# A small routed group gathered into 64 columns, ahead of a dynamic loop over (chunk, expert) pairs

## The chip, the cores and the metric

One Trainium2 chip, and of it one core. The metric is the device time of one execution in microseconds (us). The kernel before was timed in three runs, 638.36, 639.25 and 640.91 us; their median is 639.25 us.

The core has engines that run beside each other, each with its own instruction stream in fixed order: TensorE (PE, with its weight loads as PEld), VectorE (DVE), ScalarE (ACT), GpSimd (POOL) and SyncE (SP), which issues nearly all DMAs. They wait for each other through semaphores.

## The reference

Three stages in a row, all in fp32, with N = 1152 rows (2 batches of 576) of 512 values:

- *Attention with random features.* For each of 2 x 8 heads, q and k (576 x 64) go through `exp(x @ omega.T - |x|^2/2 - max)`, then `num = q_p @ (k_p.T @ v)`, `den = q_p @ sum(k_p) + 1e-6`, and the output is `num / den`. The heads side by side give a matrix x of 1152 x 512.
- *Routed experts, 8 of them.* Each row takes the one expert with the largest logit: `e = argmax(x @ w_gate)`. Its output is `gate * sigmoid(x @ w_output_gate)[e] * (relu(x @ w1[e]) @ w2[e])`, with `gate` the softmax value of e, w1 512 x 1024 and w2 1024 x 512.
- *Dense experts, 4 of them.* All rows go through all four, and the four outputs are added with weights `p = domain_probs / sum`.

Which expert a row takes is known only when the logits are there, so this is decided on the chip.

## The kernel before, in words

Values are split into a rounded part and the rest, both in the type fp32r ("rounded fp32", one pass on TensorE), and a product is made of three matmuls: high x high, high x low, low x high (`mm3`, L558). Matmuls on plain fp32 tiles (the transposes, the attention products, the gate row in `gate_row`) take two passes each in the records.

*Attention* (to about 117 us) runs by hand-written software stages over (batch, half of the heads). `stage_d` (L336) makes one normalised tile `xn` of up to 128 rows x 256 values on VectorE (L351), transposes it on TensorE (L354) and puts it, split, into `xh` and `xl`, where the 1152 rows lie as columns. There are 20 such calls. The tiles hold every fourth row of a batch, put in the order `SLOT_J`; the last 64 rows of a batch are a "rest" tile.

*Routed experts.* The 1152 columns are four chunks of 288, two for each batch: 256 from two tiles and 32 from the rest tile. For each batch the expert that most rows take is its main expert, and each chunk goes through the main expert of its batch whole, columns of other rows being multiplied with zero by the gate row. One chunk through the first layer is `unit1` (8 x 4 x 3 = 96 matmuls of 288 columns), through the second `unit2` (4 x 8 x 3 = 96 matmuls); results go to `x2T`, 512 x 1152. `extras` (L649) makes, on VectorE, the list of all other (chunk, expert) pairs that have at least one row, with their number `nx`, the experts `le` and chunks `lc`, and for each a mask in `mt`. A dynamic loop (L701 to L721) then makes one trip for each pair: the whole chunk of 288 columns through the pair's expert, with a gate row that is zero for all other rows, added to `x2T`. The order is: unit1 and unit2 of chunk 0, unit1 of chunk 1, unit2 of chunk 1, the loop, then chunks 2 and 3.

*Weights.* An expert's layer is loaded by two DMAs of 1 MB each on SP into staging tiles `st`, of which there are two in all, and split into 8 pairs of tiles (`whi` by ScalarE at L90, `wlo` by VectorE or GpSimd at L91). There are 8 tile pairs for the first layer and 8 for the second, so a tile of the next expert is split when the last matmul of the former expert has read it. The first-layer weights for the loop's first trip are asked for ahead of unit2 of chunk 1 (L694 to L696); a trip loads its own second layer and the first layer of the next trip, and the last trip loads that of batch 1's main expert. Where there is no pair, the index at L694 is that of batch 1's main expert.

*Dense experts* (from about 252 us) follow with products of 320 and 256 columns and of 512 columns, and run to the end.

*What sets the order.* The instructions are written in the order of the code, but a scheduler fixes each engine's stream before the run: at a modelled time it issues to each engine the first instruction in code order that is ready, as far as tiles of a pool are free. So instructions of later code fill modelled gaps. Nothing is moved across the bounds of the dynamic loop.

Of the kernel before, what the change touches and what calls it, by code (L numbers as in the profile page):

```python
# [9 lines left out]
F32 = mybir.dt.float32  # L10
# [12 lines left out]
DM = 512  # L23
# [6 lines left out]
HBUFS = 4  # L30
GROUPS = ((0, 320), (640, 256))
LAG, LAGD = 3, 5
EB, FLIP = 6, 1
MXS = 8
SCALE = 1.0 / (D ** 0.25)
# [4 lines left out]
def moe_stack(ctx, tc, q, k, v, omega, w_gate, w_ogate, mw1, mw2, dprobs, dw1, dw2, out):  # L40
# [3 lines left out]
    def f32(ap):  # L44
        return ap.bitcast(F32)
# [110 lines left out]
    def load_group(b, hh, cut=1):  # L156
# [7 lines left out]
        if (b, hh) == (0, 0):  # L164
            raw["q", 2] = load_rest(q, "qr")

    om2 = cp.tile([128, 2, D], F32, name="om2")
    for r in range(2):
        nc.scalar.dma_start(om2[:, r, :], omega)
# [21 lines left out]
    wgh = cp.tile([128, KB, 16], F32R, name="wgh")  # L191
    wgl = cp.tile([128, KB, 16], F32R, name="wgl")

    def prep_late():
        TT(fold, ident[:, 0:32], ident[:, 32:64], op=ALU.add)
        TT(fold, fold, ident[:, 64:96], op=ALU.add)
        TT(fold, fold, ident[:, 96:128], op=ALU.add)
        nc.vector.tensor_reduce(cmask, ident.rearrange("p (c r) -> p c r", r=32), axis=AX.X, op=ALU.add)
        nc.gpsimd.iota(i32, pattern=[[1, 32]], base=0, channel_multiplier=0)
        nc.vector.tensor_copy(iota, i32)  # L200
        TS(iota1, iota, 1.0, None, op0=ALU.add)
        TS(rev, iota[:, 0:NE], -1.0, float(NE), op0=ALU.mult, op1=ALU.add)
        nc.vector.tensor_copy(ue, iota[:, 0:NE].unsqueeze(1).to_broadcast([128, 4, NE]))
        nc.vector.tensor_copy(uc, iota[:, 0:4].unsqueeze(2).to_broadcast([128, 4, NE]))
        nc.vector.memset(lgr, 0.0)
        split(wgh, wgl, wg)
        ds_ = cp.tile([128, 9], F32, name="ds_")
        nc.vector.tensor_reduce(ds_, dpr, axis=AX.X, op=ALU.add)
        TS(ds_, ds_, 1e-9, None, op0=ALU.add)
        nc.vector.reciprocal(ds_, ds_)  # L210
        TT(pb, dpr, ds_.unsqueeze(2).to_broadcast([128, 9, NE2]), op=ALU.mult)
# [124 lines left out]
    def stage_d(b, hh, u):  # L336
# [10 lines left out]
        rd = ap.tile([128, G], F32, tag="rd", name="rd", bufs=4)  # L347
        TS(rd[:m], ps[:m, :, D], M * 1e-6, None, op0=ALU.add)
        nc.vector.reciprocal(rd[:m], rd[:m])
        xn = ap.tile([128, G, D], F32, tag="xn", name="xn")  # L350
        TT(xn[:m], ps[:m, :, 0:D], rd[:m].unsqueeze(2).to_broadcast([m, G, D]), op=ALU.mult)  # L351
        px = bank[:, 0:256].rearrange("p (g n) -> p g n", g=2)
        for g in range(2):
            nc.tensor.transpose(px[:, g, :m], xn[:m, 2 * g:2 * g + 2, :].rearrange("p a d -> p (a d)"), ident[:m, :m])  # L354
# [270 lines left out]
    def dyn(w, e):  # L625
        return w[bass.ds(e, 1)].rearrange("o a b -> (o a) b")
# [22 lines left out]
    def extras():  # L649
# [10 lines left out]
        for i, sft in enumerate((1, 2, 4, 8, 16)):  # L660
            dst = (pa, pb_)[i % 2]
            nc.vector.tensor_copy(dst[:, 0:sft], src[:, 0:sft])
            TT(dst[:, sft:32], src[:, sft:32], src[:, 0:32 - sft], op=ALU.add)
            src = dst
        nx = cp.tile([128, 1], I32, name="nx")
        nc.vector.tensor_copy(nx, src[:, 31:32])
        mine = cp.tile([128, 32], F32, name="mine")
# [4 lines left out]
        TT(mv, src.unsqueeze(1).to_broadcast([128, 32, 32]), iota1.unsqueeze(2).to_broadcast([128, 32, 32]),  # L672
           op=ALU.is_equal)
        lists = []
        for nm, tab in (("le", ue), ("lc", uc)):
            t = lp.tile([128, 32, 32], F32, tag="lt", name="lt", bufs=1)
            TT(t, mv, tab.rearrange("p c e -> p (c e)").unsqueeze(1).to_broadcast([128, 32, 32]), op=ALU.mult)
            s = cp.tile([128, 32], F32, name=nm + "f")
            nc.vector.tensor_reduce(s, t, axis=AX.X, op=ALU.add)
# [2 lines left out]
            si = cp.tile([128, 32], I32, name=nm)  # L682
            nc.vector.tensor_copy(si, s)
            lists.append(si)
        return nx, mt, lists[0], lists[1]

    E0.load2((nc.vector, nc.gpsimd))
    unit2(0, E0.w2, hs)
    nx_t, mt, le_t, lc_t = extras()
    hs = unit1(1, E0.w1)  # L690
    for c in (2, 3):
        for cols in x2cols(c):
            nc.gpsimd.memset(x2T[:, :, cols], 0.0)
    e = nc.values_load(le_t[0:1, 0:1], engines=[SP], min_val=0, max_val=NE - 1)  # L694
    E1 = Expert(dyn(mw1, e), None, nc.vector)
    E1.load1()  # L696
    unit2(1, E0.w2, hs)


    nx = nc.values_load(nx_t[0:1, 0:1], min_val=0, max_val=28)  # L700
# [238 lines left out]
```

## Time and profile before

| | us |
|---|---|
| median of the three timed runs | 639.25 |
| the profiled execution, its own time | 637.48 |
| its span in the trace | 635.7 |
| VectorE busy | 422.4 |
| ScalarE busy | 263.2 |
| GpSimd busy | 259.9 |
| mean granted TensorE clock (share of full) | 0.995 |

The span is that of one profiled execution, and lies 1.78 us under that execution's time. Busy shares are means over stages with different limits, so they say little of one stage. TensorE's matmuls overlap in the records (a record of 0.29 us may be followed by the next after 0.13 us), so the step from one start to the next is what a matmul costs, not its duration. A timeline row gives the start, the time, the engine, the line, what is written and read, the number of merged instructions, and in brackets how long the engine had been idle and what ended that.

### The profile page before, as it was taken

Reading aid. Unit: us, or ns where it says so; the run is one execution under the profiler, and the core shown is the slowest. Engines: PE = TensorE matmul, PEld = TensorE weight load, DVE = VectorE, ACT = ScalarE, POOL = GpSimd, SP = SyncE. Lnnn points to the kernel's source line nnn. Section 1 sums busy time; section 2 is a strip of 40 time slices with the busy share of each in tenths; the row PEclk is TensorE's granted clock in tenths of the full one; section 3 lists DMA queues with packets and bytes.
Section 4 is the critical chain, followed back from the end, with each engine's and each line's share of the span. In section 5 each row is a group of like instructions: output and inputs, shape, how many; then the busy total and the mean of one; then the engine's idle time right before and its main releaser. Section 6 shows DMA issues by size and latency. Waiting matters only on the chain.

```text
span 635.7 us, 10767 instructions
## 1 busy us (share of the span) xinstructions
PE 615.7 (97%) x3985; PEld 565.4 (89%) x3986; DVE 422.4 (66%) x953; ACT 263.2 (41%) x632; POOL 259.9 (41%) x297
## 2 busy tenths in 40 slices
PE   7989989899999999899999999999999999999997
PEld 6879889799998999789899899899899898898995
DVE  7677576885284478976756656666667666666564
ACT  5567474414062244544433433433343343442230
POOL 4994032500000001367636646646645745744220
PEclk9999998999999999999999999999999999999999
DMA  8711033005243302201202202102201102200004
GB/s 200 188 35 34 2 139 128 2 6 194 68 132 132 135 1 66 67 2 51 83 1 67 67 0 68 68 1 66 68 2 66 67 1 68 67 1 1 2 0 148
DMA packets 38180, 39.60 MB, mean 62 GB/s; under 512 B 14448, under 2 KB 26736, under 8 KB 38128
## 3 DMA queue, kind: packets, MB, share of 16 engines
q1 hardware_dynamic: 37840, 38.85, 19.6%
q8 instruction: 31, 0.51, 0.3%
q14 instruction: 21, 0.17, 0.1%
q10 hardware_dynamic: 288, 0.07, 0.0%
HBM read 36.55 MB, written 2.36 MB: 61 GB/s over the span
## 4 chain that ended last, share of the span: by engine, by line
PE 87%; DVE 5%; DMA 3%; ACT 2%; issue 1%; SPq 1%; POOL 0%; DVEq 0%; ACTq 0%
PE po L561 10%; PE po L560 10%; PE po L562 10%; PE pp L560 9%; PE pp L561 9%; PE pp L562 9%; PE py L560 3%; PE py L562 3%; PE py L561 3%; PE kv L297 3%; PE ph L562 3%; PE ph L560 3%; PE ph L561 3%; PE pnd L345 2%; DMA st<-in_moe_w_dram 1%
## 5 line engine op out<-in xcount | busy, mean ns | idle before, releaser
L91 POOL TENSOR_TENSOR wlo<-st,whi 128x512 fp32r<-128x512 f32 x100 | 121.5, 1236 | 243.2 <-ACT whi L90 238.9
L884 DVE SCALAR_TENSOR_TENSOR oacc<-po,pb,oacc 128x512 f32<-128x512 f32 x135 | 100.1, 748 | 56.5 <-PE po L562 56.4
L90 ACT CAST whi<-st 128x512 fp32r<-128x512 f32 x144 | 82.0, 598 | 134.2 <-PE po L562 49.3
L560 PE MATMUL po<-whi,hh 128*128 128x512 f32 x288 | 112.5, 391 | 0.0
L561 PE MATMUL po<-wlo,hh 128*128 128x512 f32 x288 | 112.4, 390 | 0.0
L562 PE MATMUL po<-whi,hl 128*128 128x512 f32 x288 | 111.9, 389 | 0.0
L556 POOL TENSOR_TENSOR hl<-c,hh 128x320 fp32r<-128x320 f32 (+1 forms) x64 | 52.5, 820 | 87.7 <-ACT hh L555 75.0
L560 PE MATMUL pp<-xh,whi 128*128 128x320 f32 (+1 forms) x256 | 75.7, 296 | 0.2 <-DVE u L843 0.2
L562 PE MATMUL pp<-xh,wlo 128*128 128x320 f32 (+1 forms) x256 | 75.8, 296 | 0.0
L561 PE MATMUL pp<-xl,whi 128*128 128x320 f32 (+1 forms) x256 | 75.7, 296 | 0.0
L562 PEld LDWEIGHTS po<-whi,hl 128*128 128x128 f32 x288 | 54.1, 188 | 11.4
L560 PEld LDWEIGHTS po<-whi,hh 128*128 128x128 f32 x288 | 54.1, 188 | 10.5
L561 PEld LDWEIGHTS po<-wlo,hh 128*128 128x128 f32 x288 | 54.1, 188 | 10.0
L831 DVE TENSOR_TENSOR c<-u,pp 128x320 f32<-128x320 f32 (+1 forms) x96 | 43.3, 453 | 22.2 <-PE pp L562 21.8
L560 PEld LDWEIGHTS pp<-xh,whi 128*128 128x128 f32 x256 | 48.5, 190 | 1.7 <-DVE u L843 0.5
L554 ACT ACTIVATE c<-c 128x320 f32<-128x320 f32 (+1 forms) x64 | 28.5, 445 | 51.3 <-DVE c L831 50.5
L561 PEld LDWEIGHTS pp<-xl,whi 128*128 128x128 f32 x256 | 48.5, 190 | 1.2
L560 PE MATMUL ph<-xh,whi 128*128 128x288 f32 (+1 forms) x160 | 47.8, 299 | 1.5 <-issue 1.5
L562 PEld LDWEIGHTS pp<-xh,wlo 128*128 128x128 f32 x256 | 48.5, 190 | 0.0
L560 PE MATMUL py<-hh,whi 128*128 128x288 f32 x160 | 48.5, 303 | 0.0
L562 PE MATMUL ph<-xh,wlo 128*128 128x288 f32 (+1 forms) x160 | 48.1, 301 | 0.0
L561 PE MATMUL ph<-xl,whi 128*128 128x288 f32 (+1 forms) x160 | 47.5, 297 | 0.0
(217 smaller groups left out, 1406.1 us busy)
## 6 DMA issues: line engine op xcount, KB each, us to landing
st<-in_moe_w_dram SPq DMA_DIRECT2D x32, 512.0 KB, 4.4
st<-in_moe_w_dram SPq DMA_DIRECT2D x12, 1024.0 KB, 5.3
v<-in_v_dram SPq DMA_DIRECT2D x16, 128.0 KB, 3.4
q<-in_q_dram SPq DMA_DIRECT2D x4, 512.0 KB, 4.7
out_dram<-oacc SPq DMA_DIRECT2D x8, 256.0 KB, 2.1
k<-in_k_dram SPq DMA_DIRECT2D x3, 512.0 KB, 5.2
k<-in_k_dram SPq DMA_DIRECT2D x4, 128.0 KB, 2.4
kr<-in_k_dram SPq DMA_DIRECT2D x2, 128.0 KB, 3.4
```

Of the source, the lines that this page charges most:

```text
L90: nc.scalar.copy(hi, src)
L91: eng.tensor_tensor(lo, src, f32(hi), op=ALU.subtract)
L297: nc.tensor.matmul(kvps[key][:, i, :], e[i][r0:r1], v65[i], start=first and i == 0, stop=last and i == G - 1)
L345: nc.tensor.matmul(ps[:m, i, :], t[:, i, c0:c0 + m], kvs[b, hh][:, i, :], start=True, stop=True)
L554: nc.scalar.activation(c, c, AF.Relu)
L556: nc.gpsimd.tensor_tensor(hl, c, f32(hh), op=ALU.subtract)
L560: nc.tensor.matmul(ps, sh_, mh, start=start, stop=False)
L561: nc.tensor.matmul(ps, sh_, ml, start=False, stop=False)
L562: nc.tensor.matmul(ps, sl_, mh, start=False, stop=stop)
L831: TT(c, u, p, op=op)
L884: STT(oacc[:, T], po, pc, oacc[:, T], op0=ALU.mult, op1=ALU.add)
```

## The change

The 20 tiles `xn` are written to a DRAM buffer `xs` too, by DMAs on SP, and `xn` has four buffers in place of two. `extras` takes the first pair out of the list where it has at most 64 rows: the list and `nx` are then shorter by one, and a mask `sel1` and the indices of its expert and chunk come back. For this pair the kernel asks for the expert's weights, reads the chunk's three stored tiles back (rows on partitions), gives every row of the pair a slot number from a running count (a matmul with an upper triangle), and gathers the rows into 64 columns by matmuls with one-hot matrices. The first layer runs with 128 moving columns, 64 high and 64 low parts side by side, so that two matmuls in place of three give a product; the second layer has these 128 columns as stationary side. The 64 results are put back to their columns, with the gate factors, by matmuls with the transposed one-hot matrices, and added to `x2T`. This stands in the code after unit1 of chunk 1 and ahead of its unit2 up to the first layer, and after it from the second layer on. The request for the first layer of the next expert (`E1.load1`) moves behind all of this. The loop itself is as it was.

```diff
+SLOTS = 64
+    xs = ctx.enter_context(tc.tile_pool(name="dp", bufs=1, space=bass.MemoryType.DRAM)).tile([9, 128, DM], F32, name="xs")
...
+    slot = cp.tile([128, SLOTS], F32, name="slot")
+    upper = cp.tile([128, 128], F32, name="upper")
+
+    def prep_slots():
+        si = cp.tile([128, 128], I32, name="si")
+        nc.gpsimd.iota(si, pattern=[[1, 128]], base=0, channel_multiplier=0)
+        nc.gpsimd.tensor_copy(slot, si[:, 0:SLOTS])
+        ui = cp.tile([128, 128], I32, name="ui")
+        nc.gpsimd.iota(ui, pattern=[[1, 128]], base=0, channel_multiplier=-1)
+        nc.gpsimd.tensor_copy(upper, ui)
+        nc.gpsimd.tensor_scalar(upper, upper, 0.0, None, op0=ALU.is_gt)
+
     def prep_late():
+        prep_slots()
...
-        xn = ap.tile([128, G, D], F32, tag="xn", name="xn")
+        xn = ap.tile([128, G, D], F32, tag="xn", name="xn", bufs=4)
         TT(xn[:m], ps[:m, :, 0:D], rd[:m].unsqueeze(2).to_broadcast([m, G, D]), op=ALU.mult)
+        dst = xs[8, 64 * b:64 * b + 64] if rest else xs[4 * b + SLOT_J[u[3]]]
+        nc.sync.dma_start(dst[:, 256 * hh:256 * hh + 256], xn[:m].rearrange("p g d -> p (g d)"))
...
+        sel = cp.tile([128, 32], F32, name="sel1")
+        STT(sel, src, 1.0, flat, op0=ALU.is_equal, op1=ALU.mult)
+        sc = cp.tile([128, 32], F32, name="sc")
+        TT(sc, sel, cnt.rearrange("p c e -> p (c e)"), op=ALU.mult)
+        few = cp.tile([128, 2], F32, name="few")
+        nc.vector.tensor_reduce(few[:, 0:1], sc, axis=AX.X, op=ALU.add)
+        TS(few[:, 0:1], few[:, 0:1], SLOTS + 0.5, None, op0=ALU.is_lt)
+        TS(few[:, 1:2], src[:, 31:32], 0.5, None, op0=ALU.is_gt)
+        TT(few[:, 0:1], few[:, 0:1], few[:, 1:2], op=ALU.mult)
+        TS(sel, sel, few[:, 0:1], None, op0=ALU.mult)
+        TT(flat, flat, sel, op=ALU.subtract)
+        TS(src, src, few[:, 0:1], None, op0=ALU.subtract)
+        where = cp.tile([128, 2], F32, name="where")
+        for i, tab in enumerate((ue, uc)):
+            TT(sc, sel, tab.rearrange("p c e -> p (c e)"), op=ALU.mult)
+            nc.vector.tensor_reduce(where[:, i:i + 1], sc, axis=AX.X, op=ALU.add)
+        wi = cp.tile([128, 2], I32, name="wi")
+        nc.vector.tensor_copy(wi, where)
...
+        pool_t = ExitStack()
+        ltp = pool_t.enter_context(tc.tile_pool(name="ltp", bufs=1))
         for nm, tab in (("le", ue), ("lc", uc)):
-            t = lp.tile([128, 32, 32], F32, tag="lt", name="lt", bufs=1)
+            t = ltp.tile([128, 32, 32], F32, tag="lt", name="lt")
...
-        return nx, mt, lists[0], lists[1]
+        pool_t.close()
+        return nx, mt, lists[0], lists[1], sel.rearrange("p (c e) -> p c e", c=4), wi
...
-    nx_t, mt, le_t, lc_t = extras()
+    nx_t, mt, le_t, lc_t, sel1, wi_t = extras()
     hs = unit1(1, E0.w1)
...
+    pool_x = ExitStack()
+    xg_ = pool_x.enter_context(tc.tile_pool(name="xg", bufs=1))
+    ex = nc.values_load(wi_t[0:1, 0:1], engines=[SP], min_val=0, max_val=NE - 1)
+    cx = nc.values_load(wi_t[0:1, 1:2], engines=[SP, DVE], min_val=0, max_val=3)
+    X = Expert(dyn(mw1, ex), dyn(mw2, ex), nc.vector)
+    X.load1()
+    xt = [xg_.tile([128, DM], F32, tag="xt", name="xt", bufs=3) for _ in range(3)]
+    for t in range(2):
+        nc.sync.dma_start(xt[t], xs[bass.ds(cx * 2 + t, 1)].rearrange("o p d -> (o p) d"))
+    nc.sync.dma_start(xt[2], xs[8])
+
+    def picked(nm, main, rest):
+
+        v = xg_.tile([128, 3], F32, name=nm)
+        t = xg_.tile([128, 4, 2, NE], F32, tag="pk", name="pk")
+        TT(t, main[:, 0:8].rearrange("p (c t) e -> p c t e", t=2),
+           sel1.unsqueeze(2).to_broadcast([128, 4, 2, NE]), op=ALU.mult)
+        nc.vector.tensor_reduce(v[:, 0:2], t.rearrange("p c t e -> p t c e"), axis=AX.XY, op=ALU.add)
+        t2 = xg_.tile([128, 4, NE], F32, tag="pk2", name="pk2")
+        TT(t2, rest, sel1, op=ALU.mult)
+        nc.vector.tensor_reduce(v[:, 2:3], t2, axis=AX.XY, op=ALU.add)
+        return v
+
+    mask, fac = picked("mask", oh_all, ohr), picked("fac", g_all, grm)
+    pr = ps_n.tile([128, 2, 3], F32, tag="nd", name="pr")
+    nc.tensor.matmul(pr[:, 0], upper, mask, start=True, stop=True)
+    nc.tensor.matmul(pr[:, 1], ones, mask, start=True, stop=True)
+    rank = xg_.tile([128, 2, 3], F32, name="rank")
+    nc.vector.tensor_copy(rank, pr)
+    for t in (1, 2):
+        for i in range(t):
+            TT(rank[:, 0, t:t + 1], rank[:, 0, t:t + 1], rank[:, 1, i:i + 1], op=ALU.add)
+    og = xg_.tile([128, 3, SLOTS], F32, name="og")
+    ogf = xg_.tile([128, 3, 2, SLOTS], F32, name="ogf")
+    for t in range(3):
+        TS(og[:, t], slot, rank[:, 0, t:t + 1], mask[:, t:t + 1], op0=ALU.is_equal, op1=ALU.mult)
+        for i in range(2):
+            TS(ogf[:, t, i], og[:, t], fac[:, t:t + 1], None, op0=ALU.mult)
+    px = ps_n.tile([128, KB, SLOTS], F32, tag="nd", name="px")
+    for kb in range(KB):
+        for t in range(3):
+            nc.tensor.matmul(px[:, kb], xt[t][:, 128 * kb:128 * kb + 128], og[:, t], start=t == 0, stop=t == 2)
+    xg = xg_.tile([128, KB, 2, SLOTS], F32R, name="xg")
+    nc.scalar.copy(xg[:, :, 0], px)
+    TT(xg[:, :, 1], px, f32(xg[:, :, 0]), op=ALU.subtract)
+    psx = ps_t.tile([128, 3, 128], F32, tag="pt", name="psx")
+    for t in range(3):
+        nc.tensor.transpose(psx[:, t], ogf[:, t].rearrange("p a s -> p (a s)"), ident)
+    back = xg_.tile([128, 3, 128], F32, name="back")
+    nc.scalar.copy(back, psx)
+
+    hx = xg_.tile([128, FB, 2, SLOTS], F32R, name="hx")
+    for q in range(2):
+        pool, tag = RINGS[q]
+        ps = pool.tile([128, 4, 2, SLOTS], F32, tag=tag, name="phx")
+        for i in range(4):
+            wh, wl = X.w1[4 * q + i]
+            for kb in range(KB):
+                nc.tensor.matmul(ps[:, i], wh[:, kb, :], xg[:, kb], start=kb == 0, stop=False)
+                nc.tensor.matmul(ps[:, i], wl[:, kb, :], xg[:, kb], start=False, stop=kb == KB - 1)
+        hl_ = xg_.tile([128, 4, SLOTS], F32, tag="hlo", name="hlo")
+        nc.scalar.copy(hl_, ps[:, :, 1])
+        TT(hl_, ps[:, :, 0], hl_, op=ALU.add)
+        hid(hl_, hx[:, 4 * q:4 * q + 4, 0], hx[:, 4 * q:4 * q + 4, 1])
+
+    unit2(1, E0.w2, hs)
+    X.load2()
+    yx = ps_j.tile([128, DM], F32, tag="pj", name="yx")
+    for f in range(FB):
+        for i in range(2):
+            nc.tensor.matmul(yx, hx[:, f], X.w2[f][i], start=f == 0 and i == 0, stop=f == FB - 1 and i == 1)
+    ys = xg_.tile([128, DM], F32, tag="xt", name="ys", bufs=3)
+    nc.scalar.copy(ys, yx)
+    for d in range(KB):
+        pa = ps_j.tile([128, 384], F32, tag="pj", name="pa")
+        nc.tensor.matmul(pa, ys[:, 128 * d:128 * d + 128], back.rearrange("p t n -> p (t n)"), start=True, stop=True)
+        for dst, src in ((bass.ds(cx * 256, 256), slice(0, 256)), (slice(1024, NX), slice(256, 384))):
+            TT(x2T[:, d, dst], x2T[:, d, dst], pa[:, src], op=ALU.add)
+    pool_x.close()
+
     e = nc.values_load(le_t[0:1, 0:1], engines=[SP], min_val=0, max_val=NE - 1)
     E1 = Expert(dyn(mw1, e), None, nc.vector)
     E1.load1()
-    unit2(1, E0.w2, hs)
```

## Rows read from the trace of the kernel before

**Rows 1.** The page: engines' busy time, and the chain that ended last by engine.
```profile
PE 615.7 (97%) x3985; PEld 565.4 (89%) x3986; DVE 422.4 (66%) x953; ACT 263.2 (41%) x632; POOL 259.9 (41%) x297
...
PE 87%; DVE 5%; DMA 3%; ACT 2%; issue 1%; SPq 1%; POOL 0%; DVEq 0%; ACTq 0%
```

**Rows 2.** Windows: stretch, length; PE, PEld, DVE, ACT, POOL busy; granted clock; DMA.
```profile
157.00:170.00 13.00, 13.00 (x98) 12.89 (x98) 3.09 (x10) 1.22 (x3) 0.00 (x0) 1.00 0.27 81
```

**Rows 3.** The instructions that read the tile `mt`: count, durations in ns, starts.
```profile
L713 DVE TENSOR_TENSOR xt<-g_all,mt x1: 225/225/225, 172.3 to 172.3; 128x64 f32<-128x64 f32 x1
```

**Rows 4.** TensorE's timeline from chunk 1's second layer to chunk 2's first.
```profile
157.22 0.65 PE L593 MATMUL pg<-dg,ones 128*128 128x288 f32 x2
...
170.50 0.29 PE L560 MATMUL ph<-xh,whi 128*128 x1
...
198.90 0.40 PE L560 MATMUL ph<-xh,whi 128*128 128x288 f32 x1 [1.52 <-issue]
```

**Rows 5.** TensorE's timeline in the dense experts: matmuls of 512 and 256 columns.
```profile
285.42 0.39 PE L560 MATMUL po<-whi,hh 128*128 128x512 f32 x1
285.65 0.39 PE L561 MATMUL po<-wlo,hh 128*128 128x512 f32 x1
...
286.45 0.28 PE L560 MATMUL pp<-xh,whi 128*128 128x256 f32 x1
286.57 0.28 PE L561 MATMUL pp<-xl,whi 128*128 128x256 f32 x1
```

**Rows 6.** The chain of waits: start, time, what (a gate row, plain fp32).
```profile
157.39 0.48 PE pg L593 x2
```

**Rows 7.** TensorE's timeline in the attention: transposes and passes of 65 columns.
```profile
60.77 0.60 PE L244 MATMUL pt<-ident,q 128*128 128x128 f32 x4
61.20 1.90 PE L345 MATMUL pnd<-kvs,qpT 128*128 128x65 f32 x16
62.91 0.36 PE L266 MATMUL pj<-omh,qTh 128*128 128x256 f32 x1
```

**Rows 8.** ScalarE's timeline: the first cast of the loop's first-layer weights.
```profile
146.38 0.62 ACT L90 CAST whi<-st 128x512 fp32r<-128x512 f32 x1 [13.75 <-DMA st<-in_moe_w_dram]
```

**Rows 9.** VectorE's timeline: list building, and splits of weights in the loop.
```profile
133.85 0.23 DVE L668 TENSOR_SCALAR mine<-iota,pa 128x32 f32<-128x32 f32 x1
134.12 0.19 DVE L669 TENSOR_TENSOR pa<-pa,fl 128x32 f32<-128x32 f32 x1
...
140.03 0.17 DVE L683 CAST le<-lef 128x32 int32<-128x32 f32 x1
...
178.45 2.50 DVE L91 TENSOR_TENSOR wlo<-st,whi 128x512 fp32r<-128x512 f32 x4
```

**Rows 10.** SP's timeline: issues of second-layer weights, two DMAs merged in each row.
```profile
93.38 9.82 SPq L113 DMA_DIRECT2D st<-in_moe_w_dram  x2
...
152.44 6.75 SPq L113 DMA_DIRECT2D st<-in_moe_w_dram  x2
```

**Rows 11.** The page, DMA issues: count, KB each, median us to landing.
```profile
st<-in_moe_w_dram SPq DMA_DIRECT2D x12, 1024.0 KB, 5.3
```

**Rows 12.** The chain of waits behind the loop's exit.
```profile
199.47 8.88 DMA st<-in_moe_w_dram
```

**Rows 13.** The instructions that write the tile `xn`.
```profile
L351 DVE TENSOR_TENSOR xn<-pnd,rd x20: 409/416/425, 32.2 to 114.4; 128x256 f32<-128x256 f32 x16, 64x256 f32<-64x256 f32 x4
```

**Rows 14.** VectorE's timeline: the 15th of these tiles.
```profile
97.42 0.42 DVE L351 TENSOR_TENSOR xn<-pnd,rd 64x256 f32<-64x256 f32 x1
```

**Rows 15.** GpSimd's timeline: its first squares, and the idle time before them.
```profile
7.16 1.20 POOL L227 TENSOR_TENSOR x<-kr 128x512 f32<-128x512 f32 x1 [5.67 <-DMA kr<-in_k_dram]
```

**Rows 16.** The page, groups: busy us, mean ns of one, idle before.
```profile
L562 PEld LDWEIGHTS po<-whi,hl 128*128 128x128 f32 x288 | 54.1, 188 | 11.4
```

**Rows 17.** Windows around a lower granted clock in the attention; columns as in rows 2.
```profile
90.00:92.00 2.00, 1.04 (x10) 0.80 (x9) 1.81 (x6) 1.90 (x7) 2.00 (x2) 1.00 0.00 0
92.00:101.00 9.00, 8.73 (x47) 7.62 (x47) 4.38 (x19) 4.53 (x14) 5.15 (x5) 0.62 0.34 117
```

## The prediction

> **What bounds the kernel now.** The page comes first. TensorE is busy for 97% of the span and the chain of waits lies on it for 87% [rows 1], so a stage is worth what it takes on TensorE plus the holes it leaves there. The reader is to look for holes, not for busy shares. Then the windows by stage: in the 13 us of the second layer of chunk 1, VectorE, ScalarE and GpSimd work 3.09, 1.22 and 0.00 us [rows 2], so this stage has room for small work on them. Then the tile view of the list `mt`: the loop's first VectorE line was executed once [rows 3], so the dynamic loop makes exactly one trip. That agrees with the reference's inputs: its gate sends all 576 rows of batch 0 to one expert, and 574 and 2 rows of batch 1 to two, and the 2 rows lie in the same half of the batch. So there is one pair off the main experts, with 2 columns of 288, and 2 is under the limit of 64.
>
> TensorE's own timeline prices it [rows 4]. The second layer of chunk 1 starts with its gate row at 157.22, the loop's first matmul at 170.50, and chunk 2 only at 198.90, after a hole of 1.52 us at the loop's exit. The 41.68 us from 157.22 to 198.90 are what the change rewrites: 13.28 us of chunk 1's second layer and 28.40 us of loop.
>
> **What goes.** With no pair left the loop makes no trip: the 28.40 us go, the hole at the exit with them.
>
> **What comes, on TensorE.** (1) First layer of the 64 columns: 8 x 4 x 2 = 64 matmuls, each with new 128x128 weights and 128 moving columns (high and low part side by side), all in rounded fp32. No row has that form with under 256 columns. From below: 512 columns follow each other every 0.23 us, 256 every 0.12 [rows 5]; a straight line through both gives 0.065 for 128, so 4.2 us. From above: the gate row is full fp32 with 288 columns and takes 0.48 us [rows 6], or 0.213 for 128 columns, so 13.7 us. In between lie single passes with new weights each time [rows 7]: four transposes of 128 columns in 0.43 us and sixteen passes of 65 columns in 1.71 us, both 0.107 us each. I take 0.107, since it is the nearest in width and in fresh weights: 64 x 0.107 = 6.85 us.
>
> The Trainium skill ("TensorE: Matmul & The Clock Gate", sections "LDWEIGHTS (loading the stationary operand)" and "Weight-path perf modes") says that a weight load costs its columns at 1.2 GHz and that fp32 weights get no fast load. That speaks against narrow matmuls here: by it an estimate is 107 ns a matmul and 6.8 us, about what the passes of rows 7 show, and a saving by the straight line would not come.
>
> (2) Gathering: 12 full-fp32 matmuls of 64 columns and 2 of 3 columns, two passes each, and 3 transposes: 24 + 4 + 3 = 31 passes at 0.107 = 3.32 us. (3) Second layer: 16 matmuls of 512 columns at 0.23 = 3.68 us. Here the columns are the stationary side, so narrowness costs nothing. (4) Scattering back: 4 full-fp32 matmuls of 384 columns, 0.48 x 384/288 = 0.64 each, 2.56 us.
>
> **What comes, beside TensorE.** Scattering waits for ScalarE's copy of the second layer's bank: the 128x512 cast takes 0.62 us [rows 8], plus 0.16 us by which a matmul's record (0.39) outlasts its step (0.23) [rows 5]: 0.78 us, with nothing left that may run. The gathering hands over from TensorE to VectorE and back: a rank copy, 3 additions, 9 one-hot operations, at 0.27 us a step [rows 9] 3.5 us, and a split of the gathered columns, near 1 us. Chunk 1's second layer needs none of it and can run in these gaps, 13.28 us of it; whether it does is set by a fixed instruction order made from modelled times. Covered it costs 0, uncovered 4.5 us; I take 1.5.
>
> The selection adds some 14 small VectorE steps after the scan (0.27 each, 3.8 us), but the first expert index is cast before the lists are built, at about 134.1 + 3.8 = 137.9 where `le` is cast at 140.03 now [rows 9]. So the first-layer weights are asked for some 2 us earlier. That gains nothing: their splits are released one by one by chunk 1's first layer, from 146.38 on [rows 8], as now. On SP three reads of the stored rows stand behind these weights, 0.75 MB; they land before 157, since the 2 MB ahead of them are being cast at 146.
>
> **What is late next: the weight stream.** Let T be the end of chunk 1's second layer, 157.22 + 13.28 + 3.32 + 6.85 + 1.5 = 182.2. The pair's second-layer weights wait in the two staging buffers until this layer frees its tiles in its last quarter; the second buffer is asked for at 159 now [rows 10], so they are there. They are split four per 2.50 us [rows 9], the first buffer free near T. Only then can the first layer of batch 1's expert be asked for: 5.3 us for 1 MB [rows 11] and a cast of 0.62, so T + 6. TensorE comes to chunk 2 at T + 3.68 + 0.78 + 2.56 = T + 7.0. The cover is about 1 us; were both halves to arrive only as the pair of loads does after the loop now, 8.88 us [rows 12], the wait would be 2.5 us.
>
> Jumping over the loop's code is not in the trace. From below 0; from above the hole of 1.52 us at today's exit [rows 4], which has a barrier in it. I take 1.0.
>
> The Trainium skill ("Runtime: NRT & Kernel Launch", section "Instruction fetch mechanics") says that instructions are fetched ahead in sequence and that a taken branch out of the fetched window waits for a fetch. No row here shows such a jump; it would put the 1.0 at its upper end.
>
> **Stored rows.** The 20 normalised tiles [rows 13] are now also written to DRAM from SP, each write holding one of four buffers. Loads on SP lie ahead of and behind them. Now SP issues the second-layer weights from 93.38 to 103.20, the second half waiting there for a buffer [rows 10]. If the writes of the four tiles before it stood behind that half, the 15th tile at 97.42 [rows 14] would wait for 103.2, 5.8 us, and for the write, an estimated 2 us for an eighth of the MB that takes 5.3 [rows 11]: 8 us. If they stand before it, 0. Their values are ready before that buffer is, so I take 0. The two constant tiles that GpSimd makes cost nothing while they fall into its idle time at the start, 5.67 us [rows 15]; without that cover its five small steps come ahead of squares that the exponentials wait for, each below the 1.20 us of a square of four times their columns: under 6 us.
>
> **Sum.** 13.28 + 3.32 + 6.85 + 1.5 + 3.68 + 0.78 + 2.56 + 1.0 = 32.97 us in place of 41.68: a gain of 8.7 us. The profiled execution takes 637.48 us, which becomes 628.8; it lies 1.8 us under the median of the three timed runs, 639.25, which becomes 630.5.
>
> **The rivals.**
> A. *The narrow matmuls run at the full-fp32 rate* (0.213): 13.7 in place of 6.85, gain 1.9, 637.4 us. For: every rounded-fp32 matmul in the kernel moves 256 columns or more, so no row excludes it. Against: the 0.107 of rows 7.
> B. *A late join.* If TensorE may pass the skipped loop only when the other engines have come to it too, it waits for all splits of batch 1's weights: second staging buffer free at T + 2.5, landed at T + 8, split at T + 10.5. That is 3.5 us past T + 7.0, of which 1.0 is in the sum: 633.0 us; with a later load, 635.5. Against: TensorE enters the loop now without a hole [rows 4].
> C. *Writes behind the weights on SP* (above): 8 us of the gain goes, 638.5 us.
> D. *Slower: weight loads that don't hide.* Should each of the 64 matmuls pay its weight load, 188 ns [rows 16], and then its 0.213 in series, the first layer takes 25.7 us, 18.8 more than forecast: 649.3 us. It decides from 0.243 us a matmul on, where the gain is gone. Against it stand the passes of rows 7, where loads do hide behind 65 columns.
> E. *The loop runs all the same*, because the pair is not taken out: 18.7 us are added to today's stage, 658 us. Only a wrong count would do that.
> F. *The clock.* From 92 to 101 us the granted clock was 0.62 [rows 17], partly at the lower level (1.2 GHz), after some 2 us in which TensorE did 1.04 us of work. A hole of that size around the skipped loop would cost a similar stretch, 9 x 0.38 = 3.4 us: 634 us.
>
> **How the numbers follow.** Forecast 0.57, A 0.20, B and F together 0.12, C 0.03, D 0.04, E and the rest 0.04. About 0.5% (3.2 us) is what a measurement of this kernel can tell from no change. Faster than 636.05: the forecast, B and F, and the cheaper part of A (0.05): 0.74. Within: the rest of A (0.15) and most of C: 0.17. Slower: D, E and the rest, and the dear part of C: 0.09. The range: with 0.065 a matmul, no hand-over hole and a free jump the gain is 8.7 + 2.7 + 1.5 + 1.0 = 13.9, so 625; the upper end takes in A and its neighbours, 638. The forecast's own range is 626 to 634.
>
> **What would show it.** The step between the 64 new matmuls: 0.107 right, 0.2 or more is A or D. No loop line executed. Chunk 2's first matmul near 190 in place of 198.90. A hole there over 2 us, ended by a weight split, is B, and a granted clock under 1 after it F. The 15th normalised tile much later than 97.42 is C. It is wrong if the last stage, from chunk 2 on, changes its own length.

## The result, and the profile after

The forecast was 630.5 us, faster. The changed kernel takes 642.56 us, median of 20 runs (637.37 to 644.38), against 639.27 us for the kernel before on the same chip (20 runs): ratio 1.0052, 95% interval 1.0031 to 1.0073. It is slower by half a per cent. The profiled execution took 642.43 us with a span of 640.6 us, 4.9 us above the span before.

The page of the changed kernel, against [rows 1]: TensorE's busy time fell by 4.0 us only, while the span grew by 4.9, so there are nearly 9 us more of holes.

```profile
PE 611.7 (95%) x3910; PEld 560.5 (87%) x3911; DVE 425.0 (66%) x974; ACT 263.1 (41%) x630; POOL 260.0 (41%) x302
```

**The rewritten stage.** TensorE's timeline of the changed kernel, against [rows 4] (start, us, what, and in brackets the idle time before it and what ended it):

```profile
163.89 0.28 PE L760 MATMUL pr<-mask,upper 128*128 128x3 f32 x2
...
167.05 2.56 PE L776 MATMUL px<-og,xt 128*128 128x64 f32 x22
...
170.53 0.33 PE L793 MATMUL phx<-xg,whi 128*128 128x128 f32 x1
...
177.73 0.70 PE L610 MATMUL pg<-dg,ones 128*128 128x288 f32 x2
...
188.01 0.40 PE L805 MATMUL yx<-whi,hx 128*128 128x512 f32 x1
...
192.56 2.85 PE L810 MATMUL pa<-back,ys 128*128 128x384 f32 x8 [0.68 <-ACT ys L807]
201.69 0.61 PE L577 MATMUL ph<-xh,whi 128*128 128x288 f32 x1 [6.28 <-DVEq L821]
202.10 0.44 PE L578 MATMUL ph<-xl,whi 128*128 128x288 f32 x1
202.34 0.44 PE L579 MATMUL ph<-xh,wlo 128*128 128x288 f32 x1
```

The loop's body was not executed. The 64 narrow matmuls follow each other every 0.11 us (170.53 to 177.73). But there is a hole of 6.28 us in front of chunk 2, and behind it the steps are 0.24 us instead of 0.13. In this hole VectorE still splits weights for the loop's expert, until 200.66; behind that the chain of waits has 0.87 us for which it names nothing:

```profile
196.36 4.30 DVE L92 TENSOR_TENSOR wlo<-st,whi 128x512 fp32r<-128x512 f32 x7
```

```profile
200.83 0.87 issue
```

The stage takes 201.69 - 163.89 = 37.80 us: 3.88 less than before, where 8.7 less were forecast.

**The stage starts late.** It starts at 163.89 instead of 157.22. Two holes ahead of it account for that. The first is at the start of the kernel. GpSimd's timeline of the changed kernel, against [rows 15]:

```profile
7.07 1.04 POOL L242 TENSOR_TENSOR x<-kr 128x512 f32<-128x512 f32 x1 [5.51 <-DMA kr<-in_k_dram]
8.06 0.24 POOL L202 CAST slot<-si 128x64 f32<-128x64 int32 x1
...
10.55 0.15 POOL L214 IOTA i<- 128x32 int32 x1
```

In the kernel before, GpSimd makes this last index row at 1.08 us:

```profile
1.08 0.16 POOL L199 IOTA i<- 128x32 int32 x1
```

VectorE, and then TensorE, in the changed kernel:

```profile
10.74 0.23 DVE L215 CAST iota<-i 128x32 f32<-128x32 int32 x1 [3.68 <-POOL i L214]
10.89 0.41 DVE L192 TENSOR_TENSOR oml<-omT,omh 128x256 fp32r<-128x256 f32 x1
```

```profile
11.35 0.58 PE L282 MATMUL pj<-oml,qTh 128*128 128x256 f32 x1 [4.26 <-DVE oml L192]
```

The constant tiles were not done in GpSimd's idle time. Only their first step was; the others stand behind the first squares, and behind them stands the old 32-column index row. VectorE waits for that row, and the split of the random features (`oml`), next in its queue, waits with it though it needs nothing from GpSimd. TensorE then waits 4.26 us, and the granted clock was 0.50 from 11 to 16 us. The first normalised tile comes at 37.4 instead of 32.2 us [rows 13], the last at 119.6 instead of 114.4.

The second hole is at the gate of batch 1, on VectorE and TensorE:

```profile
124.41 1.25 DVE L608 TENSOR_SCALAR dg<-fold,sel 128x32 f32<-128x32 f32 x1
125.58 0.31 DVE L607 TENSOR_SCALAR dg<-ident,sel 128x128 f32<-128x128 f32 x1
...
126.38 1.29 DVE L607 TENSOR_SCALAR dg<-ident,sel 128x128 f32<-128x128 f32 x1
127.59 0.23 DVE L608 TENSOR_SCALAR dg<-fold,sel 128x32 f32<-128x32 f32 x1
...
128.34 0.17 DVE L398 COPY lgr<-lgp 16x32 f32<-16x32 f32 x1
```

```profile
128.56 0.23 PE L404 MATMUL lgt<-ident,lgr 16*128 16x16 f32 x1 [1.91 <-DVE lgr L398]
```

The kernel before waits 0.64 us ahead of the first of these transposes, and not at all ahead of the last one:

```profile
120.03 0.29 PE L387 MATMUL lgt<-ident,lgs 16*128 16x16 f32 x2 [0.64 <-DVE lgr L381]
...
122.05 0.23 PE L387 MATMUL lgt<-ident,lgr 16*128 16x16 f32 x1
```

The windows behind the three holes of the changed kernel (stretch, length; busy time of PE, PEld, DVE, ACT, POOL; granted clock; DMA share, GB/s):

```profile
11.00:16.00 5.00, 4.50 (x20) 4.15 (x20) 3.94 (x14) 1.14 (x4) 3.13 (x4) 0.50 1.14 269
126.00:135.00 9.00, 7.09 (x42) 6.83 (x42) 8.63 (x26) 3.26 (x9) 4.15 (x3) 0.81 0.00 0
201.00:206.00 5.00, 4.31 (x18) 4.31 (x19) 1.63 (x7) 0.41 (x1) 0.00 (x0) 0.50 0.62 218
```

At 0.50 TensorE is at its lower level (1.2 GHz). The balance of the two profiled executions: 6.67 us later into the stage, 3.88 us gained in it, 438.91 us from chunk 2 to the end instead of 436.80, 2.11 lost, most of it at the lower clock from 201 on. 6.67 - 3.88 + 2.11 = 4.9 us, the difference of the spans. Of the 13.6 us by which this execution lies above its forecast (642.43 against 628.8), 6.67 lie ahead of the stage, 4.83 in it (37.80 instead of 32.97) and 2.11 behind it.

### The profile page after: what moved, and what is told of

Its sections match the earlier page's. It is cut to its first block, busy times and chain, and to the rows that moved or that the text cites. A ratio compares the mean times of both kernels' runs of the same rounds, so it can differ in the third digit from the quotient of the medians.

```text
span 640.6 us, 10594 instructions
## 1 busy us (share of the span) xinstructions
PE 611.7 (95%) x3910; PEld 560.5 (87%) x3911; DVE 425.0 (66%) x974; ACT 263.1 (41%) x630; POOL 260.0 (41%) x302
## 4 chain that ended last, share of the span: by engine, by line
PE 65%; DVE 3%; issue 1%
PE po L578 10%; PE po L577 10%; PE po L579 10%; PE pp L577 9%; PE pp L578 9%; PE pp L579 9%; PE ph L577 2%; PE ph L578 1%; PE ph L579 1%; PE py L577 1%; PE py L579 1%; PE py L578 1%; DVE xcl L92 1%; DVE c L951 0%; DVE x2T L640 0%
## 5 line engine op out<-in xcount | busy, mean ns | idle before, releaser
L298 ACT ACTIVATE e<-pj,nb 128x128 f32<-128x128 f32 x144 | 41.4, 381 | 18.1 <-DVE nb L291 18.1
L577 PE MATMUL ph<-xh,whi 128*128 128x288 f32 x128 | 40.2, 314 | 6.3 <-DVEq L821 6.3
L568 DVE SCALAR_TENSOR_TENSOR hl<-c,hh 128x320 fp32r<-128x320 f32 (+1 forms) x64 | 44.6, 728 | 0.3
L579 PE MATMUL ph<-xh,wlo 128*128 128x288 f32 x128 | 40.0, 313 | 0.0
```

Of the source, the lines that this page charges most:

```text
L298: nc.scalar.activation(e[:, i // 2, i % 2], ps[:, i // 2, i % 2], AF.Exp, bias=nb[:, i // 2, i % 2:i % 2 + 1])
L568: STT(hl, src, 0.0, f32(hh), op0=ALU.max, op1=ALU.subtract)
L577: nc.tensor.matmul(ps, sh_, mh, start=start, stop=False)
L579: nc.tensor.matmul(ps, sl_, mh, start=False, stop=stop)
```

## The experiments

Single executions of one kernel scatter by up to 9 us, and the granted clock with them, so medians are compared and the holes are read in the profiles. The kernels were run beside the kernel before, whose medians there were 639.25, 639.10, 638.89 and 638.80 us. Theories: S, the constant tiles in GpSimd's queue; J, TensorE waits at the skipped loop for VectorE's splits (the prediction's B). Rivals: W, the stored rows; L, the loop's own instructions.

**1. The constant tiles last in the preparation.**

```diff
 def prep_late():
-    prep_slots()
     TT(fold, ident[:, 0:32], ident[:, 32:64], op=ALU.add)
 ...
     TT(pb, dpr, ds_.unsqueeze(2).to_broadcast([128, 9, NE2]), op=ALU.mult)
+    prep_slots()
```

> Edit: the call that makes the two constant tiles on GpSimd moves to the end of prep_late, so that the 32-column index row comes ahead of them in GpSimd's order. Theory S (start): VectorE waits at 7 us for that index row and holds back the low part of omega, so TensorE stands 4.26 us and then runs at the lower clock; then the hole goes, the granted clock of 11 to 16 us is 1.00 again, the first normalised tile comes near 32.2 instead of 37.4, and the time falls by 5 to 6.5 us, to about 636.5. Rival W (stored rows): the 20 writes on SP delay the attention; then the tiles stay late and the time stays within 1 us of the changed kernel's 642.5.

Measured: 637.34 us (12 runs), 5.2 less than the changed kernel; ratio to before 0.9975 (0.9947 to 1.0003). Its start, on TensorE:

```profile
8.72 0.39 PE L282 MATMUL pj<-oml,qTh 128*128 128x256 f32 x1 [1.44 <-DVE oml L192]
```

The holes at the gate (1.82 us) and at the loop (6.35 us) are still there. The price of S is right; one expectation failed in this profile: the granted clock from 11 to 16 us was 0.71, not 1.00 (it was 1.00 in runs 3 and 7).

**2. The loop left out** (the change as it is, without the loop; it makes no trip on these inputs).

```diff
-nx = nc.values_load(nx_t[0:1, 0:1], min_val=0, max_val=28)
-with tc.For_i(0, nx, 1) as it:
-    ...
```

> Edit: the dynamic loop is left out (for these inputs it makes no trip). Theory J (join): TensorE waits at the skipped loop until VectorE has come to it too, behind all eight splits of batch 1's first-layer weights (end at 200.66); without the loop chunk 2 starts at about 195.5, as soon as the first pair of tiles is split, 6 us earlier, the clock does not fall behind it (some 2 us more), and the time falls by 7 to 8 us, to about 635. Rival L (late weights): the weights themselves are what it waits for; then chunk 2 starts no earlier than about 200 and the time stays within 1.5 us of 642.5.

Measured: 634.89 us (6 runs), 7.7 less than the changed kernel; ratio to before 0.993 (0.991 to 0.9949). TensorE goes from the scatter to chunk 2 without a hole, and at the full clock:

```profile
192.65 0.40 PE L805 MATMUL yx<-wlo,hx 128*128 128x512 f32 x1
193.72 2.85 PE L810 MATMUL pa<-back,ys 128*128 128x384 f32 x8 [0.67 <-ACT ys L807]
196.11 0.59 PE L577 MATMUL ph<-xh,whi 128*128 128x288 f32 x1
...
196.67 0.32 PE L579 MATMUL ph<-xh,wlo 128*128 128x288 f32 x1
```

The stage, from its first matmul at 165.03, is 31.08 us here. The time fits J; but without the loop neither the meeting nor the loop's own instructions are left, so L was not ruled out by this run. This run alone doesn't tell them apart; run 5 does.

**3. Both.** Edits 1 and 2 together.

> Both edits: constant tiles last, and no loop. S and J together: the gains add, about 629 to 630, which is what the prediction's sum gives without its term for the jump. If one cause hides the other (the attention's delay being taken up by a wait behind it), less than 10 us in all.

Measured: 631.34 us (6 runs), 11.2 less than the changed kernel, ratio to before 0.9864 (0.9835 to 0.9894). The two gains, 5.2 and 7.7, nearly add. Without the late index row and without the loop the change is worth 7.9 us, where the forecast without its jump gives 9.7 (8.7 + 1.0).

**4. The kernel before with the constant tiles alone** (made first in the preparation, used by nothing).

```diff
 def prep_late():
+    prep_slots()
     TT(fold, ident[:, 0:32], ident[:, 32:64], op=ALU.add)
```

> Edit: the kernel before with nothing but the two constant tiles added, at the head of prep_late as in the changed kernel. Theory S: the whole delay of the start comes from them: the same hole near 7 us, and 4.5 to 6 us more than before, about 644.5. Rival W: 639.3, no change, since no row is stored.

Measured: 641.67 us (12 runs), ratio 1.0045 (1.0022 to 1.0069): 2.4 us slower, half of what was expected. The hole itself is there in full:

```profile
11.34 0.58 PE L281 MATMUL pj<-oml,qTh 128*128 128x256 f32 x1 [4.70 <-DVE oml L191]
```

The direction is shown by adding the tiles alone; why 4.7 us of hole cost 2.4 in the median here and 5.2 in run 1 is open.

**5. The loop's weights earlier.** The first-layer load of the loop's expert moves ahead of chunk 1's second layer, so that VectorE has no splits left when the loop is reached.

```diff
+E1 = Expert(dyn(mw1, e), None, nc.vector)
+E1.load1()
 unit2(1, E0.w2, hs)
 X.load2()
 ...
-E1 = Expert(dyn(mw1, e), None, nc.vector)
-E1.load1()
 nx = nc.values_load(nx_t[0:1, 0:1], min_val=0, max_val=28)
```

> The changed kernel with one block moved: the first-layer load of the loop's expert (its index, the two DMAs and the eight casts and splits) stands ahead of the second layer of the main expert's chunk 1 instead of behind the small expert's scatter. The loop stays. If the 6.28 us hole ahead of chunk 2 is the skipped loop waiting for VectorE, which still has seven of those splits to do (theory J), the splits now lie in 174 to 183 us, the hole is 1.0 to 1.5 us, chunk 2 begins some 5 us earlier, the granted clock behind it stays at 1.00, and the time is 5 to 7 us under the changed kernel's (about 636). If the loop's own instructions cost the hole (theory L: register loads, branch, code), it stays over 5 us and the time is within 1.5 us of the changed kernel's. A third way: the small expert's second layer now comes behind these weights in staging, its matmuls (at 188 us) wait for it, and half or more of the gain goes there.

Measured: 640.81 us (12 runs), 1.75 less than the changed kernel; ratio to before 1.0029 (1.0003 to 1.0054). VectorE and TensorE in this kernel:

```profile
193.95 2.55 DVE L815 TENSOR_TENSOR x2T<-x2T,pa 128x256 f32 x8 [2.26 <-PE pa L813]
198.29 0.48 DVE L607 TENSOR_SCALAR dg<-ident,sel 128x128 f32<-128x128 f32 x2 [1.79 <-issue]
```

```profile
193.00 2.85 PE L813 MATMUL pa<-back,ys 128*128 128x384 f32 x8 [0.68 <-ACT ys L810]
200.74 0.47 PE L577 MATMUL ph<-xh,whi 128*128 128x288 f32 x1 [4.89 <-issue]
```

VectorE's last work ahead of the loop ends at 196.5 and it is past the loop at 198.29. TensorE comes out only at 200.74, after 4.89 us for which nothing in the profile can be named. In the changed kernel TensorE came out 1.03 us behind VectorE's last split (201.69 against 200.66), here 4.24 us behind VectorE's last work. So two waits lie side by side in the changed kernel: the meeting with VectorE (J), which ends last there, and the loop's own instructions (L), for which 4.89 us of idle time are left with VectorE's splits done early. By estimate J alone would hold TensorE for over 5 us too, from the end of its scatter at 195.41 to 200.66. So J is real but is not the whole cause, and taking it away shortens the hole by 1.4 us only (6.28 to 4.89).

**6. Edits 1 and 5 together, the loop kept.**

> Both repairs with the loop kept: the load of the loop's expert moved as in the run before, and the constant tiles made last in the preparation. If the two causes are separate and complete, the time is the sum of what each gave: 637.3 (tiles last alone) less 5 to 7, so 630.5 to 632.5, level with the kernel that had the tiles last and no loop (631.34); if the loop costs by itself, 635 or more.

Measured: 636.69 us (12 runs), ratio 0.9959 (0.9928 to 0.9989): no sum of two gains, and 5.35 above run 3. The hole at the loop is 4.84 us.

**7. Run 6, with the gate's copy on ScalarE.**

```diff
-nc.vector.tensor_copy(lgr[:, 32 * cc:32 * cc + 32], ps[:, 256:NC])
+nc.scalar.copy(lgr[:, 32 * cc:32 * cc + 32], ps[:, 256:NC])
```

> The run before with one more edit: the copy of the gate's rest columns (lgr) is ScalarE's instead of VectorE's. Every kernel with the whole change waits 1.8 to 1.9 us at the gate's last transpose for this copy, which stands on VectorE behind five builds of gate rows; before, the wait was 0.64. If this hole and the clock behind it are the rest of the loss, the hole falls under 0.7 us, the granted clock from 126 to 135 us comes back towards 1.00, and the time falls by 1.5 to 3 us (about 629.5). If the copy only trades places on ScalarE, or the order of the attention moves with it, the time stays within 1 us.

Measured: 635.53 us (12 runs), ratio to before 0.9948 (0.9921 to 0.9976). The hole at the gate's last transpose is gone and the granted clock from 125 to 140 us is 1.00, but of the 1.5 to 3 us expected from it the median shows 1.2, less than what the scatter of 12 executions (631.55 to 639.32 us) can tell from nothing. The hole at the loop is the one of run 5:

```profile
183.71 0.40 PE L808 MATMUL yx<-wlo,hx 128*128 128x512 f32 x1
184.78 2.85 PE L813 MATMUL pa<-back,ys 128*128 128x384 f32 x8 [0.68 <-ACT ys L810]
192.69 0.61 PE L577 MATMUL ph<-xh,whi 128*128 128x288 f32 x1 [5.06 <-issue]
...
193.34 0.44 PE L579 MATMUL ph<-xh,wlo 128*128 128x288 f32 x1
```

With run 10 (634.95 us), from which it can't be told apart, this is the fastest of the kernels that keep the whole loop: 0.5% under the kernel before, 1.1% under the changed one.

**8. The kernel before with the stored rows alone.**

```diff
+dst = xs[8, 64 * b:64 * b + 64] if rest else xs[4 * b + SLOT_J[u[3]]]
+nc.sync.dma_start(dst[:, 256 * hh:256 * hh + 256], xn[:m].rearrange("p g d -> p (g d)"))
```

> The kernel before with only the stored rows: the 20 DMAs of the normalised attention rows to the scratch in DRAM, and four buffers for them instead of two; nothing reads them. Theory S (the constant tiles and the late join are the whole loss): within 1 us of the kernel before, and the wait at the gate's last transpose stays near 0.64 us. Rival W (the writes take SP's and the DMA engines' time from weights and loads, or shift VectorE's order at the gate): 1.5 to 3 us slower, with the wait at the gate's transpose near 1.9 us or first-layer weights later by more than 2 us.

Measured: 640.42 us (12 runs), ratio 1.0025 (0.9993 to 1.0058): not told from nothing. TensorE waits 2.55 us for `oml` at the start, 0.68 before, but that lies ahead of the first stored row. At the gate's last transpose it waits where the kernel before does not:

```profile
125.13 0.23 PE L390 MATMUL lgt<-ident,lgr 16*128 16x16 f32 x1 [1.97 <-DVE lgr L384]
```

So the gate's hole comes with the stored rows and their four buffers. By which way is not shown: VectorE's order at the gate is another one, and GpSimd, which clears `x2T` ahead of its splits there, now starts on that only when a write of a stored row is done (14.24 us idle, ended by the DMA `xs<-xn`), 2.70 us behind the last tile instead of 1.46. The time says only that it is small.

**9. The loop with a tiny body** (run 7, all of the body left out but one small VectorE copy).

> The kernel with both repairs and ScalarE's gate copy (635.53 us), its loop kept with count and branch, but its body, which never runs here, cut to one small VectorE copy. In that kernel TensorE waits 5.1 us for nothing that the profile shows between the small expert's scatter and chunk 2, with all of chunk 2's weights ready. Theory B (the price is the jump over a long body, whose far side the engine has to fetch): the wait falls under 2.5 us and the time by 2.5 to 4.5 us. Theory R (the price is fixed: the count's load into a register, the meeting of the engines, the branch): the wait stays at 4 to 5.5 us and the time within 1 us.

Measured: 634.91 us (10 runs). The chain of waits at the loop (start, time, what):

```profile
187.58 5.36 DMA st<-in_moe_w_dram
192.94 0.90 issue
```

With nothing in the body that uses the main expert's second layer, its weights are asked for ahead of the loop (at 184.74), though this load stands behind the loop in the code; so here the statement that nothing is moved across the bounds of the loop does not hold. By the chain, the meeting at the loop waits for their transfer. The hole is 5.64 us, but for a new reason, so the time decides nothing. Nor do the last 0.90 us price the short body: the changed kernel, with its whole body, has 0.87 us at this place.

**10. The count loaded early** (run 7, the loop's count brought to the registers ahead of chunk 1's second layer).

```diff
+nx = nc.values_load(nx_t[0:1, 0:1], min_val=0, max_val=28)
 E1.load1()
 unit2(1, E0.w2, hs)
 ...
-nx = nc.values_load(nx_t[0:1, 0:1], min_val=0, max_val=28)
```

> The same kernel with its whole body, and the loop's count loaded into the engines' registers ahead of chunk 1's second layer on the main expert, some 15 us earlier, instead of at the loop. Theory R in its cheapest form (the load of the count from memory into TensorE's register is what takes the time): the wait at the loop falls by 1.5 to 3 us, and a hole of under 1 us comes up where the load now stands, so 1 to 2.5 us less in all. Theory B: the wait stays within 0.7 us of 5.1, and the time is equal or up to 1 us longer.

Measured: 634.95 us (10 runs); the hole is unchanged:

```profile
199.21 0.61 PE L577 MATMUL ph<-xh,whi 128*128 128x288 f32 x1 [5.00 <-issue]
```

The load of the count is not what takes the time.

**11. The loop without matmuls in its body** (run 7; what follows from the matmuls is left out too).

```diff
-    hs = l1(E1.w1, xhc, xlc, *RINGS)
 ...
-    add_out(xe.w2, hs, gate_row(sx), ...)
```

> The same kernel with the loop's body kept for all engines but without its matmuls and what follows them (the pair's first and second layer and the adding of its rows, which never run here); TensorE's own part of the loop is left with the branch alone, SyncE, ScalarE and VectorE keep most of theirs. Theory B with TensorE's own code as the price: the wait falls as with the tiny body, under 2.5 us. If another engine's jump is what TensorE waits for, the wait stays over 4 us here and falls only with the tiny body.

Measured: 625.19 us (4 runs), ratio to before 0.9817 (0.9761 to 0.9873), 10.3 less than run 7. TensorE:

```profile
180.74 0.40 PE L808 MATMUL yx<-wlo,hx 128*128 128x512 f32 x1
182.69 0.40 PE L577 MATMUL ph<-xh,whi 128*128 128x288 f32 x1 [1.55 <-ACT ys L810]
...
183.06 2.75 PE L813 MATMUL pa<-back,ys 128*128 128x384 f32 x8
185.35 0.59 PE L579 MATMUL ph<-xh,wlo 128*128 128x288 f32 x1
```

The copy and the scatter now come behind the loop, though they stand ahead of it in the code, and the wait ends with ScalarE's copy; so 1.55 us is at most TensorE's own, and the fair measure is from the last matmul ahead of the copy to the third matmul of chunk 2: 185.35 - 180.74 = 4.61 us. In run 7 it is 193.34 - 183.71 = 9.63, without a loop (run 2) 196.67 - 192.65 = 4.02. The 10.3 us of the medians (4 and 12 runs) are more than the loop: of the 8.5 us between the two profiled spans (622.6 and 631.1), 5.0 are this passage, 3.0 lie ahead of it, where the last normalised tile comes at 112.0 instead of 115.0, and 0.5 behind it.

**12. Half of the matmuls** (run 7; the body keeps the pair's first layer, its second layer and what follows left out).

> The kernel with both repairs and ScalarE's gate copy (635.53 us), and in the loop's body, which never runs here, the pair's second layer, its gate row and the adding of its rows left out: TensorE keeps the first layer's 96 matmuls there, about half of its part. With the whole body TensorE's wait at the loop was 5.06 us, without any matmul in it 1.55 (0.59 of it ScalarE's copy of the small expert's rows, which there comes after the loop). If the price goes with the length of what is jumped over, the wait is 2.7 to 3.9 us and the time about 630; if it is one price for any code that is not at hand, it stays at 4.5 to 5.5 us (about 634.5); if half the body still counts as at hand, it falls to 1 to 2 us (about 626).

Measured: 629.04 us (4 runs), ratio 0.9849 (0.9796 to 0.9903). TensorE:

```profile
181.61 0.40 PE L808 MATMUL yx<-wlo,hx 128*128 128x512 f32 x1
184.06 0.40 PE L577 MATMUL ph<-xh,whi 128*128 128x288 f32 x1 [2.06 <-ACT ys L810]
...
184.43 4.44 PE L813 MATMUL pa<-back,ys 128*128 128x384 f32 x8
188.41 0.59 PE L579 MATMUL ph<-xh,wlo 128*128 128x288 f32 x1
```

188.41 - 181.61 = 6.80 us. Over the kernel without a loop the passage is 0.6 us longer with no TensorE matmul in the body, 2.8 with half of them and 5.6 with all. But 1.7 of the 2.8 are the scatter's eight passes, stretched from 2.75 to 4.44 us at a granted clock of 0.66 from 184 to 189 us, while run 7's lower clock comes behind the passage. By TensorE's idle time alone the four kernels have 0.67 us (no loop), 1.55, 2.06 and 5.74 (0.68 and 5.06), and in runs 11 and 12 the wait ends with ScalarE's copy. So taking the second half of the matmuls out of the body removes over 3 us of idle time, taking out the first half too at most some 0.5 more. A price in step with the length is not shown: the wait is nearest to the third way of the expectation (half the body still at hand), the time to the first.

That TensorE's own part of the loop is what costs is likely, since VectorE is past the loop 2.4 to 2.6 us ahead of TensorE in runs 5, 6, 7 and 10. But runs 11 and 12 also leave out what ScalarE and VectorE do for the pair's layers, so the engines are not fully separated.

What part of it is fetching code is only argued. The DMA queues (queue and kind: packets, MB, share of 16 engines) show a transfer of instructions by queue 8 in run 7 from 188 to 190 us and in run 12 from 182 to 184 us, inside their holes, and none by that queue from 178 to 186 in run 11. First run 7, then run 12:

```profile
q8 instruction: 1, 0.02, 3.7%
```

```profile
q8 instruction: 1, 0.02, 3.5%
```

It is 0.02 MB, so its own transfer doesn't fill 5 us, and one such transfer goes with a hole of 5.06 us in run 7 and of 2.06 in run 12. The Trainium skill ("Runtime: NRT & Kernel Launch", section "Instruction fetch mechanics") says that a taken branch whose target lies outside the fetched window stalls for a fetch; that runs 7 and 12 have a transfer in the hole and run 11 has none agrees with it. What else lies in the 5 us is open.

## Why the prediction was wrong

- **The narrow first layer: right.** 64 steps of 0.11 us, 7.2 us in place of 6.85. Rivals A and D fall. The Trainium skill's estimate ("TensorE: Matmul & The Clock Gate", section "LDWEIGHTS (loading the stationary operand)"), 107 ns a matmul, lies some 5% under it.
- **Gathering, second layer, scatter: right.** 0.109 us a pass (22 in 2.40 us), 0.23 a step of 512 columns, 0.87 in place of 0.78 for the copy (from 188.01 + 3.68 to 192.56), and 2.39 in place of 2.56 for the scatter (run 2, 193.72 to 196.11).
- **Hand-over, 1.5 us: too dear.** The main expert's second layer fills the gaps, and 163.89 to 188.01 is 24.12 us where the terms give 24.95. Without the loop the stage is 31.08 us, 10.6 less than before; the forecast without its jump gives 31.97. E didn't happen, nor did C: the tiles come an even 5.2 us late.
- **The jump over the loop, 1.0 us: the first wrong step.** Measured 4.89 us with all data ready, 6.28 with the late join, and a lower clock behind it. The bound from above, 1.52 us, was taken from the exit after a trip; in the kernel before no loop is skipped, so no row held the case. Rival B is there as it was described: TensorE waits for VectorE's splits until 200.66. But it lies beside the jump, and without it 4.89 us are left, which B did not contain. B was set aside because TensorE enters the loop without a hole; that was a loop that is entered. What makes up the 4.89 us stays open; the body's matmuls belong to it (run 12: at most 2.06 us with half of them).
- **The constant tiles, 0 us: the second wrong step.** The cover was argued from GpSimd's idle time, without following which step waits for what behind them. The price named there without that cover, under 6 us, holds, but by another way than the squares: the index row that VectorE needs early was made at 1.08 us and now stands behind them (10.55). Cost: 4.26 us of hole; 5.2 us in the median by run 1, 2.4 by run 4.
- **Stored rows, 0 us: unclear.** Run 8 has 1.3 us more than the kernel before, with an interval that holds 0. With them TensorE waits 1.97 us at the gate's last transpose, where before it waits 0.64 us at the first.
- **The clock, F: real, at three places.** In the changed kernel it fell behind the three holes. The prediction's own sign of being wrong, a changed length from chunk 2 on, came true with 2.11 us.

## What to carry to other kernels

A new step costs what stands behind it in its engine's queue: follow the first consumer of the next instruction, not the engine's idle share. A loop that makes no trip is not free: here TensorE stood some 5 us with the whole body skipped and 2 with half of its matmuls, so it can pay to keep the body that a common case skips short on the engine that bounds. Leaving a thing out shows its total price but not its cause; only making the weights ready early told the meeting from the jump. And where two waits lie side by side, taking one away gains only what it outlasts the other by.

## What the runs showed that was not expected

- A loop that makes one trip is left after 1.52 us [rows 4]; the same loop skipped holds TensorE for 4.8 to 5.1 us (runs 5, 6, 7 and 10).
- By the chain of waits, the meeting at a loop waited for a DMA in flight that nothing in the loop used (run 9, 5.36 us).
- The granted clock stayed at 1.00 after holes of 0.64, 0.68 and 1.52 us (before), 1.55 us (run 11) and 1.82 us (run 1, at the gate). It was below it after 1.91 us (0.81 from 126 to 135 us), 2.06 us (run 12, 0.66 from 184 to 189 us), 4.26 and 6.28 us (0.50 from 11 to 16 and from 201 to 206 us).
- VectorE's builds of 32 and 128 columns took 1.25 and 1.29 us while GpSimd split weights, and 0.23 and 0.31 us in the other rows. The two slow ones make, by estimate, some 2 us of the gate copy's lateness; no run tests it. GpSimd's timeline of the changed kernel at that place, against VectorE's rows of the gate above:

```profile
124.31 1.31 POOL L92 TENSOR_TENSOR wlo<-st,whi 128x512 fp32r<-128x512 f32 x1
...
125.77 1.81 POOL L92 TENSOR_TENSOR wlo<-st,whi 128x512 fp32r<-128x512 f32 x1
```
